# Chunk-selected attention with an ELU MLP on one core: the first block of 384 queries cut into two halves of 192

## The chip, the cores and the metric

The kernel runs on one core of one Trainium2 chip. The metric is the device time of one execution in microseconds (us), as the median over repeated executions. The time before the change is 292.71 us.

## What is computed

The reference is an attention over q, k and v of shape (4, 8, 768, 64) followed by an MLP over 3072 tokens of 512 features, everything given and returned in float32.

```
ub   = sum_d max(q*k_min, q*k_max)        # per query and chunk of 32 keys, 24 chunks
top  = the 6 chunks with the largest ub (chunks after the query's own are excluded)
s    = q @ k.T / 8, kept where the key is not after the query and its chunk is in top
attn = softmax(s) @ v                     # per head
x    = attn, heads side by side           # (3072, 512)
h    = x @ w_in                           # (3072, 2048)
g    = h if h > 0 else exp(h) - 1         # ELU
out  = g @ w_out                          # (3072, 512)
```

A query among the first 192 of its batch (6 chunks of 32) has at most six chunks that are not after it. All of them are in `top`, so for these queries only the causal rule is left.

## The kernel before

**Blocks.** The work is cut into eight blocks (b, h): batch b in 0..3 and half h in 0..1 of its 768 positions, 384 queries each (`HS`). Block i = 2b + h is an attention block and then an MLP block of the same 384 tokens. Heads are taken in four pairs r = 0..3.

**One pair's preparation** (`prep`, with `load`). Six loads of 96 KB bring K, Q and V of the pair's two heads, 384 rows each, into the buffers `kf`, `qf`, `vf`. TensorE transposes K and Q (L468). VectorE takes minimum and maximum of each chunk (L488). `put` (L474 on ScalarE, L476 on VectorE, L478 on GpSimd) makes the bf16 operands `lhs` (keys) and `rhs` (queries) of the scores. A constant pattern of chunks (`econst`, L455/L457) fills the upper half of `lhs` in the first two batches; the selection's mask fills the upper half of `rhs`. One matmul therefore gives the scores with unselected chunks pushed far down. GpSimd casts V into `vext` (L576).

**Selection** (`select`), for two pairs together: the bound as a matmul (L595 in batch 0, L602 later), a transpose (L614), the eight largest per query (L623), a comparison with the sixth (L629), a transpose back (L635), and a copy of the mask into `rhs` (L643, in the operation named `mk`). In blocks with h = 0 it covers only queries 192 to 383.

**Attention** (`attend`) of one pair: scores in segments of key tiles (L673; in the first block a further matmul L678 adds the causal triangle, in later blocks VectorE multiplies by a triangle at L704/L713), exponentials (L689/L695), the product with V (L734), reciprocal and scaling (L745/L748). The result `on` is transposed to `xt`: in the first three blocks by TensorE and a VectorE copy (L769/L772), from the fourth by a DMA transpose on SyncE's queue (L756; the parameter `dx`).

**MLP** (`mlp`): for each of 16 slices of 128 features four matmuls of 384 columns accumulate over the four pairs' `xt` (L784), then exp on ScalarE (L792), min/-1 on GpSimd (L796) and the combination on VectorE (L800) give `gT`. The slices need `xt` of all four pairs. Then for three tiles of 128 tokens sixteen matmuls of 512 columns (L811) give the output, which is copied (L819/L821) and stored. `w_in` and `w_out` are each brought in four DMAs by GpSimd's queue with a cast to bf16 (`load_w_in` L377, `load_w_out` L384). The list `gate` says after how many casts of V each of the eight is issued.

**Order.** A planner (`Graph.run`) lays out all operations at build time with assumed durations, priorities (`att_prio`, `mlp_prio`) and buffer counts (the table `T`), and the program is emitted in the order it found. On the chip each engine runs its list strictly in that order. Where the planner saw TensorE idle it placed an operation `fill` of two matmuls of zeros (L842); a fill is part of TensorE's list and takes its time whether or not it is needed. At most eight loads are under way at once: each load from SyncE's or ScalarE's queue waits for the eighth before it. Eight Q loads, those of the first four pairs, are issued from ScalarE's queue at the start (`nfirst=4`), all other loads from SyncE's.

Of the kernel before, what the change touches and what calls it, by code (L numbers as in the profile page):

```python
# [40 lines left out]
T = dict(kf=6, qf=4, vf=6, pt=10, xt=9, gT=26, xq=2, rhs=7, nfirst=4, vlate=4.68,  # L41
         gate=[2, 3, 5, 5, 6, 6, 8, 10], attw=[7.68, 8.15], mlp=[10.21, 8.14], loada=0.01,
         prepa=4.24, sela=0.01, fill=40, cold=6, evo=0.01, mf=0.3, dx=3,
         slk=[133.66, 359.3, 1054.91, 138.27], sf=0.95, us=1, tp=1, es=0, d1=0)
# [22 lines left out]
class Graph:  # L67
# [41 lines left out]
    def run(self, at=None, dma_lat=(700.0, 900.0)):  # L109
# [8 lines left out]
        flying = [0, 0]  # L118
# [27 lines left out]
        def transfer(t):  # L146
# [3 lines left out]
            while True:  # L150
# [9 lines left out]
                for r, _ in live:  # L160
                    if r[0][1] <= 1e-6:
                        o = r.pop(0)[2]
                        flying[o.engine != POOL] -= 1
                        o.finish = dma_at + dma_lat[1] + o.slack
                        settle(o)
# [9 lines left out]
        while left or any(rings.values()):  # L175
# [13 lines left out]
            while moved:  # L189
                moved = False  # L190
                for e in engines:
# [5 lines left out]
                    while i < len(lst):  # L197
# [4 lines left out]
                        ok = o.xfer is None or e == POOL or flying[1] < 8  # L202
# [32 lines left out]
                    else:  # L235
                        flying[e != POOL] += 1
# [40 lines left out]
def kernel(  # L277
# [45 lines left out]
    slots("gT", T["gT"], [P, HS], BF16)  # L323
# [21 lines left out]
    def consts():  # L345
# [23 lines left out]
        for t in store["selb"]:  # L369
            nc.vector.memset(t, 0.0)  # L370
        for t in store["vext"]:
            nc.gpsimd.memset(t[:, :, :, D:D + 1], 1.0)
# [54 lines left out]

    def load(b, h, r, prio):
# [3 lines left out]
        for buf, src, late in ((kf, k, 0.0), (qf, q, 0.001), (vf, v, T["vlate"])):  # L432
# [9 lines left out]
    def prep(b, h, r, prio):  # L442
# [54 lines left out]
        for hd, rows in enumerate((lo, hi)):  # L497
            put("ka", lambda hd=hd: ap(lb)[lo, hd, ts], lambda rows=rows: ap(kt)[rows],
                c_half(dve=265, pool=560), [(kt, 0)], [(lb, (h, hd))], prio + T["evo"])
# [57 lines left out]
        else:  # L557
# [21 lines left out]
            reads=[(vf, 0), (vf, 1)], writes=[(vx[b, r], h)], prio=prio + T["vlate"]))  # L579

    def select(b, h, gr, prio):
# [56 lines left out]
        for j in range(2):  # L638
            rb = rhs[b, h, prs[j]]

            def mk(e, rb=rb, j=j):
                eng = nc.vector if e == DVE else nc.gpsimd
                eng.tensor_copy(out=ap(rb)[hi, :, q0:HS],  # L643
                                in_=ap(sT)[64 * j:64 * j + 64, 0:nq].rearrange("p (a q) -> p a q", a=1)
                                .to_broadcast([64, 2, nq]))
            g.op("mk" + tag, c_half(dve=2 * nq / 3.84 + 175),
                 mk, reads=[(sT, 0)], writes=[(rb, "mask")], prio=prio, port=True)

    early = [[(0, 0, 128, 0)], [(0, 128, 256, 0), (1, 128, 256, 256)], [(2, 256, 128, 0)]]
# [4 lines left out]
    def attend(b, h, r, prio, w):  # L654
# [4 lines left out]
        todo = early if 2 * b + h < T["es"] and h == 0 else steps[h]  # L659
        nst = len(todo)  # L660
        for si, segs in enumerate(todo):
# [18 lines left out]
            for hd in range(2):  # L680
# [4 lines left out]
                     + ([(ls, ("e", hh)) for hh in range(h + 1)] if b < 2 else []) + [(rs, hd)] + ([(rs, "mask")] if max(c + wd for _k, c, wd, _p in segs) > Q0 else []),  # L685
# [42 lines left out]
        for hd in range(2):  # L728
            def pv(e, hd=hd):
                for qi in range(3):  # L730
# [11 lines left out]
                 writes=[(o3, hd)], prio=pr)  # L742
        rcp, on = g.buf("rcp"), g.buf("on")
        g.op("rcp" + tag, {DVE: (110, 190)},
             lambda e: nc.vector.reciprocal(out=ap(rcp), in_=o3v()[:, :, :, D:D + 1]),  # L745
             reads=[(o3, 0), (o3, 1)], writes=[(rcp, 0)], prio=pr)
        g.op("on" + tag, c_dve(HS),
             lambda e: nc.vector.tensor_tensor(  # L748
                 out=ap(on)[:, :, :, :].rearrange("p q h d -> p h q d"), in0=o3v()[:, :, :, 0:D],
                 in1=ap(rcp)[:, :, :, :].to_broadcast([P, 2, 3, D]), op=AOT.mult),  # L750
             reads=[(o3, 0), (o3, 1), (rcp, 0)], writes=[(on, 0)], prio=pr)
        xt = g.buf("xt")
        xT[b, h, r] = xt
        if 2 * b + h >= T["dx"]:
            def tx(e):
# [3 lines left out]
            g.op("tx" + tag, {SP: (1310, 1310)}, tx, reads=[(on, 0)], writes=[(xt, 0)], prio=pr - 20.0,  # L759
                 xfer=600.0, slack=T["slk"][3])  # L760
            return
        bx = g.buf("bank")

# [3 lines left out]
        def px(e):  # L767
            for qi in range(3):
                nc.tensor.transpose(pxt()[:, P * qi:P * (qi + 1)], ap(on)[:, qi, :, :], ident_b)  # L769
        g.op("px" + tag, c_mm([P] * 3), px, reads=[(on, 0)], writes=[(bx, 0)], prio=pr)  # L770
        g.op("xt" + tag, {DVE: (275, 360)},
             lambda e: nc.vector.tensor_copy(out=ap(xt), in_=pxt()),  # L772
             reads=[(bx, 0)], writes=[(xt, 0)], prio=pr)

    def mlp(i):
        b, h = divmod(i, 2)
        gts = []
        for fc in range(NFC):
            pr = mlp_prio(i, T["mf"] * fc / NFC)
            bank = g.buf("bank")  # L780

            def mm1(e, bank=bank, fc=fc):
                for kk in range(NKK):
                    nc.tensor.matmul(ap(bank)[:, 0:HS], lhsT=w_in_sb[:, kk, P * fc:P * (fc + 1)],  # L784
                                     rhs=ap(xT[b, h, kk]), start=(kk == 0), stop=(kk == NKK - 1))
            g.op(f"h{i}.{fc}", c_mm([HS] * 4), mm1,
                 reads=[(xT[b, h, kk], 0) for kk in range(NKK)] + [(fixed, ("wi", fc // 4))],
                 writes=[(bank, 0)], prio=pr)
            eb, mb, gt = g.buf("e"), g.buf("m"), g.buf("gT")
            gts.append(gt)  # L790
            g.op(f"e{i}.{fc}", c_act(HS),
                 lambda e, eb=eb, bank=bank: nc.scalar.activation(out=ap(eb), in_=ap(bank)[:, 0:HS],  # L792
# [97 lines left out]
```

## Time and profile before

| quantity | value |
|---|---|
| median of 7 runs | 292.71 us (292.4 to 293.96) |
| the profiled execution's own time | 292.6 us |
| its span | 290.9 us |
| TensorE busy | 282.5 us, 97% of the span |
| ScalarE, VectorE, GpSimd busy | 226.9, 216.1, 153.0 us |
| granted TensorE clock over the span | 0.999 |
| HBM read, written | 27.26 MB, 6.29 MB |
| first MLP matmul starts at | 39.0 us |
| last output matmul starts at | 285.8 us |

The 1.7 us between time and span lie outside the profiled instructions. "Busy" of TensorE is the union of records that overlap, and it includes the fills of zeros, so 97% does not say that 97% of the span is useful work. Matmul durations in the profile include the pass through the array; what one costs in a stream is the distance from one start to the next (a row "x4" of 0.65 us has four matmuls 0.162 us apart).

### The profile page before, as it was taken

The numbers are of one execution on the slowest core, as the hardware profiler recorded it, in microseconds if no ns is written. First come the engines' busy times: TensorE is split into PE (matmuls) and PEld (weight loads), VectorE is DVE, ScalarE is ACT, GpSimd is POOL, SyncE is SP. The second block draws the span as 40 slices with busy tenths as digits, with TensorE's granted clock in tenths as the row PEclk, the third lists the DMA queues.
The fourth block names the chain that finished last, engine by engine and source line by source line (L and its number), as shares of the span: only waits on it lengthen the run. The fifth ranks groups of instructions, "written<-read, shape, count | busy, mean of one in ns | idle before, by whom it ended". The sixth has DMA issues, their size and how long they took to land.

```text
span 290.9 us, 7004 instructions
## 1 busy us (share of the span) xinstructions
PE 282.5 (97%) x2288; PEld 170.6 (59%) x2316; DVE 216.1 (74%) x649; ACT 226.9 (78%) x495; POOL 153.0 (53%) x345
## 2 busy tenths in 40 slices
PE   8799999999999999999999999999999999999996
PEld 4467556656565557656565556656665566655542
DVE  8596869897788779777888889778899777623800
ACT  2599799989897699997896799988797978736610
POOL 7585546643489757644485527723385415404700
PEclk9999999999999999999999999999999999999999
DMA  8989998896776785233422523134100210011010
GB/s 169 206 165 220 168 210 156 169 193 133 207 180 147 196 199 123 62 102 99 118 66 68 155 78 71 29 87 108 53 14 18 86 52 14 16 50 75 0 72 37
DMA packets 92836, 31.79 MB, mean 109 GB/s; under 512 B 85632, under 2 KB 89728, under 8 KB 92800
## 3 DMA queue, kind: packets, MB, share of 16 engines
q1 hardware_dynamic: 85376, 26.36, 37.6%
q0 software_dynamic: 4224, 4.19, 9.2%
q10 hardware_dynamic: 3200, 0.79, 1.4%
q8 instruction: 18, 0.29, 0.4%
q14 instruction: 18, 0.15, 0.2%
HBM read 27.26 MB, written 6.29 MB: 115 GB/s over the span
## 4 chain that ended last, share of the span: by engine, by line
PE 87%; DVE 5%; DMA 3%; ACT 2%; issue 1%; ACTq 1%
PE bank L784 28%; PE bank L811 27%; PE bank L673 11%; PE bank L734 7%; PE bank L468 6%; PE bank L842 3%; PE bank L602 2%; DVE kmm L488 2%; DMA qf<-in_q_dram 1%; PE bank L595 1%; DMA vf<-in_v_dram 1%; ACTq L424 1%; ACT pt L689 1%; PE bank L769 1%; DVE thr L623 1%
## 5 line engine op out<-in xcount | busy, mean ns | idle before, releaser
L796 POOL TENSOR_SCALAR m<-e 128x384 f32<-128x384 f32 x128 | 65.3, 522 | 63.9 <-ACT e L792 54.0
L811 PE MATMUL bank<-w_out_sb,gT 128*128 128x512 bf16 x360 | 91.6, 379 | 1.3 <-issue 0.2
L784 PE MATMUL bank<-xt,w_in_sb 128*128 128x384 bf16 x512 | 91.2, 326 | 0.3 <-ACT xq L474 0.2
L800 DVE SCALAR_TENSOR_TENSOR gT<-bank,m 128x384 bf16<-128x384 f32 x128 | 67.3, 554 | 20.7 <-POOL m L796 18.5
L689 ACT ACTIVATE pt<-bank 128x384 bf16<-128x384 f32 (+1 forms) x160 | 75.2, 550 | 7.3 <-PE bank L673 6.4
L784 PEld LDWEIGHTS <-w_in_sb 128*128 128x128 bf16 x512 | 49.2, 98 | 31.9 <-issue 1.9
L792 ACT ACTIVATE e<-bank 128x384 f32<-128x384 f32 x128 | 60.7, 506 | 8.8 <-PE bank L784 6.8
L811 PEld LDWEIGHTS <-gT 128*128 128x128 bf16 x384 | 36.1, 98 | 34.2 <-issue 1.9
L673 PE MATMUL bank<-rhs,lhs 128*128 128x384 bf16 (+2 forms) x288 | 52.9, 290 | 0.1
L478 POOL COPY lhs<-kt 64x384 bf16<-64x384 bf16 x57 | 29.8, 523 | 34.2 <-ACT kt L474 31.9
L488 DVE TENSOR_REDUCE kmm<-bank 128x12 f32<-128x384 f32 x64 | 33.7, 546 | 5.9 <-ACT kt L474 5.2
L673 PEld LDWEIGHTS <-lhs 128*128 128x128 bf16 x288 | 25.5, 98 | 17.5 <-issue 1.8
L819 ACT ACTIVATE o<-bank 128x512 f32<-128x512 f32 x21 | 12.5, 597 | 20.2 <-PE bank L811 18.5
L734 PEld LDWEIGHTS <-pt 128*128 128x128 bf16 x672 | 24.5, 98 | 5.6 <-issue 1.2
L474 ACT ACTIVATE xq<-bank 64x384 f32<-64x384 f32 (+1 forms) x47 | 22.6, 484 | 5.0 <-PE bank L468 3.8
L734 PE MATMUL bank<-vext,pt 128*128 128x65 bf16 x672 | 25.7, 193 | 0.1
L842 PE MATMUL bank<-zeros 128*128 128x512 bf16 x76 | 22.5, 416 | 1.5 <-DVE half L348 1.3
L478 POOL CAST rhs<-xq 64x384 bf16<-64x384 f32 x35 | 18.3, 523 | 8.2 <-ACT xq L474 4.3
L695 ACT ACTIVATE pt<-bank 128x512 bf16<-128x512 f32 x32 | 19.6, 614 | 2.3 <-PE bank L673 2.3
L474 ACT ACTIVATE kt<-bank 128x384 bf16<-128x384 f32 x29 | 14.2, 490 | 6.4 <-PE bank L468 6.4
L576 POOL TENSOR_SCALAR vext<-vf 128x384 bf16<-128x384 f32 x32 | 16.6, 530 | 3.9 <-DMA vf<-in_v_dram 2.4
L748 DVE TENSOR_TENSOR on<-bank,rcp 128x384 bf16<-128x384 f32 x32 | 17.7, 554 | 0.8
(67 smaller groups left out, 271.4 us busy)
## 6 DMA issues: line engine op xcount, KB each, us to landing
kf<-in_k_dram SPq DMA_DIRECT2D x64, 96.0 KB, 2.7
vf<-in_v_dram SPq DMA_DIRECT2D x64, 96.0 KB, 2.6
out_dram<-o SPq DMA_DIRECT2D x24, 256.0 KB, 2.1
qf<-in_q_dram SPq DMA_DIRECT2D x56, 96.0 KB, 2.5
w_in_sb<-in_moe_w_in_dram POOLq DMA_DIRECT2D x4, 512.0 KB, 8.9
w_out_sb<-in_moe_w_out_dram POOLq DMA_DIRECT2D x4, 512.0 KB, 8.6
qf<-in_q_dram ACTq DMA_DIRECT2D x8, 96.0 KB, 3.4
xt<-on SPq DMA_TRANSPOSE x20, 2.3
```

Of the source, the lines that this page charges most:

```text
L474: nc.scalar.activation(out=dst(), in_=src(), func=AF.Copy)
L478: nc.gpsimd.tensor_copy(out=dst(), in_=src())
L488: nc.vector.tensor_reduce(out=ap(kmm)[:, w, :], in_=ap(bank)[:, 0:HS].rearrange("p (c w) -> p c w", w=CHUNK), axis=AX.X, op=op)
L673: nc.tensor.matmul(ap(banks[hd])[:, o + pc:o + pc + wd], lhsT=ap(ls)[:, hd, P * kb:P * (kb + 1)], rhs=ap(rs)[:, hd, c0 - HS * h:c0 - HS * ...
L689: lambda e, hd=hd, pt=pt, banks=banks, wtot=wtot: nc.scalar.activation(out=ap(pt)[:, hd, 0:wtot], in_=ap(banks[hd])[:, 0:wtot], func=AF.Ex ...
L734: nc.tensor.matmul(o3v()[:, hd, qi, :], lhsT=ap(pt)[:, hd, off:off + P], rhs=ap(vx[b, r])[:, kb, hd, :], start=(kb == 0), stop=(kb == qt))
L784: nc.tensor.matmul(ap(bank)[:, 0:HS], lhsT=w_in_sb[:, kk, P * fc:P * (fc + 1)], rhs=ap(xT[b, h, kk]), start=(kk == 0), stop=(kk == NKK - 1))
L792: lambda e, eb=eb, bank=bank: nc.scalar.activation(out=ap(eb), in_=ap(bank)[:, 0:HS], func=AF.Exp),
L796: lambda e, eb=eb, mb=mb: nc.gpsimd.tensor_scalar(out=ap(mb), in0=ap(eb), scalar1=-1.0, scalar2=1.0, op0=AOT.add, op1=AOT.mult),
L800: lambda e, gt=gt, bank=bank, mb=mb: nc.vector.scalar_tensor_tensor(out=ap(gt), in0=ap(bank)[:, 0:HS], scalar=0.0, in1=ap(mb), op0=AOT.max ...
L811: nc.tensor.matmul(ap(bank), lhsT=ap(gts[fc])[:, P * tt:P * (tt + 1)], rhs=w_out_sb[:, fc, :], start=(fc == 0), stop=(fc == NFC - 1))
L842: nc.tensor.matmul(ap(bank), lhsT=zeros[:, 0:P], rhs=zeros, start=True, stop=True)
```

## The change

The first attention block (b = 0, h = 0) is handled by a new function `attend_first`. Each pair is done in two parts: queries 0 to 191, which read no selection mask, and queries 192 to 383, which read it. Each part has its own exponentials, product with V, scaling, TensorE transpose and copy into its half of `xt`. Part 0 has earlier priorities (`a0`, `m0`). The first MLP block is computed in the same halves: one PSUM bank holds two feature slices of 192 tokens each instead of one slice of 384; `gT` becomes a buffer of two slices. The causal triangle is added by matmul in the first two blocks (`tp=2`, before 1), and the DMA transpose starts with the second block (`dx=1`, before 3). Only the first two pairs' Q and K loads are issued first (`nfirst=2`); Q of pairs 2 and 3 moves to SyncE's queue. The table `T` changes throughout: fewer load buffers (K 3 for 6, Q 3 for 4, V 2 for 6), other priorities, and other gates of the weight loads (0, 4, 4, 8, 9, 10, 11, 11 for 2, 3, 5, 5, 6, 6, 8, 10). The planner now models the limit of eight loads by the eighth load before. The mask copy may go to ScalarE in the first block (`fx=2`).

```diff
-T = dict(kf=6, qf=4, vf=6, pt=10, xt=9, gT=26, xq=2, rhs=7, nfirst=4, vlate=4.68,
-         gate=[2, 3, 5, 5, 6, 6, 8, 10], attw=[7.68, 8.15], mlp=[10.21, 8.14], loada=0.01,
-         prepa=4.24, sela=0.01, fill=40, cold=6, evo=0.01, mf=0.3, dx=3,
-         slk=[133.66, 359.3, 1054.91, 138.27], sf=0.95, us=1, tp=1, es=0, d1=0)
+T = dict(kf=3, qf=3, vf=2, pt=8, xt=20, gT=12, xq=6, rhs=5, nfirst=2, vlate=0.74,
+         gate=[0, 4, 4, 8, 9, 10, 11, 11], attw=[8.27, 7.58], mlp=[13.11, 8.2], loada=0.01,
+         prepa=4.3, sela=0.01, fill=45, cold=11, evo=0.01, mf=0.35, dx=1,
+         slk=[129.81, 382.99, 1057.96, 99.72], sf=0.9, us=1, tp=2, d1=2, m0=39.0, a0=34.0, vl0=6.5,
+         fx=2)
...
-                        ok = o.xfer is None or e == POOL or flying[1] < 8
+                        ok = (o.xfer is None or e == POOL or len(issued) < 8
+                              or (issued[-8].finish or 1e12) - issued[-8].slack <= t)
...
+    def attend_first(r, prio, w):
+        tag = f"00{r}"
+        ls, rs = lhs[0, r], rhs[0, 0, r]
+        parts = (([(0, 0, Q0, 0), (1, P, 64, Q0)], [(0, P, 0), (Q0, 64, 0)],
+                  [[(0, 0)], [(0, P), (1, Q0)]]),
+                 ([(0, Q0, Q0, 0), (1, Q0, Q0, Q0), (2, 2 * P, P, 2 * Q0)], [(Q0, 64, 64), (2 * Q0, P, 0)],
+                  [[(0, 0), (1, Q0)], [(0, 64), (1, Q0 + 64), (2, 2 * Q0)]]))
+        for part, (segs, diag, tiles) in enumerate(parts):
+            pr = prio + w * 0.5 if part else prio - T["a0"]
+            pt = g.buf("pt" if part else "pa")
...
+                     reads=[(ls, (0, hd)), (ls, ("e", 0)), (rs, hd)] + ([(rs, "mask")] if part else []),
...
+            turn(0, 0, r, o3, 2, part + 1, pr)
...
+        for f2 in range(NFC // 2):
+            if i:
...
+                continue
+            for part in range(2):
+                pr = mlp_prio(0, T["mf"] * f2 / (NFC / 2)) - (0 if part else T["m0"])
+                bank = g.buf("bank")
+                for x in range(2):
+                    mm1(bank, 2 * f2 + x, Q0 * x, Q0 * part, Q0, x, pr)
...
-            for _ in range(2):
+            for _ in range(1 if cold else 2):
                 nc.tensor.matmul(ap(bank), lhsT=zeros[:, 0:P], rhs=zeros, start=True, stop=True)
-        cost = 860 if i < T["cold"] else 432
+        cost = 430 if cold else 432
```

## The prediction

> **What bounds the kernel now.** I read the page's busy shares and slices first, then busy time by stage, then who waits for whom in the first 40 us, then the DMAs in two stretches, then the timeline. From the page (engine, busy us, share; then 40 slices of 7.3 us in tenths):
>
> ```profile
> span 290.9 us, 7004 instructions
> PE 282.5 (97%) x2288; PEld 170.6 (59%) x2316; DVE 216.1 (74%) x649; ACT 226.9 (78%) x495; POOL 153.0 (53%) x345
> ...
> ACT  2599799989897699997896799988797978736610
> ...
> DMA  8989998896776785233422523134100210011010
> ```
>
> TensorE is the bound after the start. ScalarE is nearly full from slice 3 to slice 8, and the DMA engines are full to about 60 us. By stage (busy us of PE, PEld, DVE, ACT, POOL; clock; DMA share; GB/s):
>
> ```profile
> 0.00:14.50 14.50, 11.62 (x50) 6.29 (x50) 9.71 (x31) 5.62 (x12) 8.88 (x35) 1.00 0.96 187
> 14.50:39.00 24.50, 23.91 (x212) 15.43 (x215) 19.50 (x76) 22.27 (x47) 17.21 (x36) 1.00 1.01 186
> 39.00:56.00 17.00, 16.89 (x157) 10.58 (x157) 15.14 (x45) 16.57 (x38) 8.60 (x18) 1.00 0.95 179
> 56.00:76.00 20.00, 19.01 (x186) 11.69 (x189) 15.95 (x48) 17.45 (x38) 9.83 (x22) 1.00 0.85 160
> 76.00:286.00 210.00, 208.76 (x1680) 125.77 (x1698) 155.75 (x452) 164.41 (x363) 108.46 (x236) 1.00 0.33 86
> ```
>
> After 76 us TensorE is idle 1.2 us in 210, so only the first 76 us have time to give. Their busy share hides zeros. The groups of the first 60 us show it (loads of weights are counted in full; four matmul records are missing):
>
> ```profile
> L842 PEld LDWEIGHTS <-zeros 128*128 128x128 bf16 x64 | 6.3, 106 | 6.3 <-issue 2.5 <-DVE half L348 1.3
> ```
>
> 64 matmuls of zeros at 0.216 us (start to start) are 13.8 us, all ahead of the first MLP matmul at 39.0 us. The waits from 5 to 40 us (waiter <- releaser: us, times, longest):
>
> ```profile
> POOL lhs L478 <- ACT kt L474: 4.0, 2, 2.6
> DVE kmm L488 <- ACT kt L474: 3.5, 2, 2.8
> ACT xq L564 <- DMA vf<-in_v_dram: 3.2, 1, 3.2
> ```
>
> ScalarE stands 3.2 us before the relu at 10.77 because its queue holds the eighth Q load until a V load (the eighth before it) has landed. GpSimd and VectorE wait behind it, and TensorE stands 0.86 and 0.76 us. Last, the DMA issues between 8 and 18 us and between 19 and 29 us (KB, median us to landing):
>
> ```profile
> vf<-in_v_dram SPq DMA_DIRECT2D x7, 96.0 KB, 2.7
> kf<-in_k_dram SPq DMA_DIRECT2D x6, 96.0 KB, 2.7
> ...
> w_in_sb<-in_moe_w_in_dram POOLq DMA_DIRECT2D x2, 512.0 KB, 7.9
> kf<-in_k_dram SPq DMA_DIRECT2D x4, 96.0 KB, 6.3
> qf<-in_q_dram SPq DMA_DIRECT2D x4, 96.0 KB, 6.6
> ```
>
> Loads issued beside two weight DMAs land 4 us later than the others.
>
> **The change part by part.** Durations are of the profiled execution (292.6 us, span 290.9; the median is 0.1 above). Counts are from the two programs' instruction lists.
>
> *TensorE's content ahead of the last output product.* Fills: 70 before, 65 after (14 stand behind it, 10 before): -5 x 0.216 = -1.08. Products with V: 16 more of 65 columns at 0.030 = +0.48. Triangles: from 24 of 128 columns to 40 of 128 and 16 of 64: +16 x 0.056 + 16 x 0.031 = +1.39. Transposes of `on`: from 36 to 16: -1.12. Scores recut in the first block: +0.05. First MLP block: 64 matmuls of 384 columns (0.162) become 128 of 192; 192 columns are not in the trace and lie midway between 128 (0.056) and 256 (0.109), 0.0825: 10.56 for 10.37, +0.19. Sum -0.1. The list is no shorter; any gain must come from waits.
>
> Here a rule speaks against the change. Matmuls of 65 columns, each with its own weight load, are 0.030 us apart (rows "x30" of 0.91 us), those of 512 columns 0.216. The Trainium skill, "TensorE: Matmul & The Clock Gate", section "Back-to-back issue gap", says that in a stream of weight loads and matmuls both set the spacing, about 81 ns at 128 columns and 131 at 512. An estimate from it, on the line between, is 89 ns at 192 and 114 at 384: 11.4 for 7.3, +4.1 us, and the forecast would be 294.8. I take +0.19, since the trace has the weight load hidden even at 65 columns; bounds 0 and +4.1.
>
> *Waits up to the first MLP matmul.* Before: content 17.0 + 13.8 of fills = 30.8, start at 39.0, so 8.2 us are lost: 1.26 before the first matmul, 2.7 at the cold start (ten fills at 0.43 for 0.216, two transpose groups at 0.85 instead of 0.49), 4.2 in waits. After: content 15.4 + 11.0 (51 fills) = 26.4. The start costs 1.26 + 2.5 again (nine fills). Two waits change:
> - ScalarE issues four Q loads instead of eight, none held: its 3.2 us stand goes. The Q loads of pairs 2 and 3 go to SyncE's queue behind K loads, at 0.53 us each; they cost nothing while the transposes that read them come later in TensorE's list (content 7.8 and 10.6, estimated landing 8.5 and 10.3 us).
> - The first weight DMA has no gate and is GpSimd's first work after the constants. It occupies GpSimd for about 0.9 us (row L377: 0.75 to 0.98), from 7.8 to 8.7. Queued behind it are the two casts of K (L478, 0.5 each) that the first scores read, ready at 9.2 and 9.7. TensorE reaches these scores at content 3.8 + 1.26 + 2.5 = 7.5: it waits about 2.2. ScalarE's next copies wait for the Q transpose behind these scores.
>
> I put the later waits of the start at 0.5 (bounds 0 and 2.0, what is now lost beyond those named). Lost: 1.26 + 2.5 + 2.7 = 6.5 for 8.2: -1.7; the first MLP matmul starts at about 32.9.
>
> *ScalarE as a check.* Its list up to the last exp of the first MLP block has 44.5 us of work before and ends at 56.1; after it is 47.3 (more scores of the second block come ahead). Before it started at 5.4 (table loaded) and lost 6.2, 3.2 of them at that load. After it can start at 4.3 and loses 3.0: 54.6, where TensorE's content is 60.6, as before at 56.1 (60.7). That is -1.5. Both say the same; I take -1.7.
>
> *Edits with no price of their own.* VectorE gains four more reciprocals, scalings and copies (4 x about 0.6) and loses the eight `xt` copies of blocks 1 and 2 (0.36 each) and the four triangles of the second block (0.72): about -3.3 of 216, at 75 to 90% busy. Split outputs of `gT` and the wider `pa` cost as the present rearranged ones (L748, 554 ns, as L800); bound 0 to +0.3. Eight more DMA transposes take SyncE's queue 1.2 us each and land in 2.3 (row of `xt`), 10 us before the MLP that reads them by TensorE's list; beside weight DMAs they may take 7, still covered. If SyncE holds there, loads queue behind it, and with three K buffers the cover is two pairs. The mask copy on ScalarE is one operation of 0.45. The fills behind the last product end near 289.0, when the last store lands: 0 to +0.2.
>
> Sum: -0.1 - 1.7 = -1.8: 290.8 of 292.6, as a median 290.9.
>
> **The rivals.**
>
> *The gain is given back between 33 and 76 us* (chance 0.18). ScalarE is 97% busy from 39 to 56 us and has more in its list there; with K, Q, V buffers halved, less is loaded ahead. If about 1.5 of the 1.8 comes back as waits, the time is 292.4. For it: 1.0 us of idle TensorE now between 56 and 76. Against: ScalarE's list ends earlier by my sum.
>
> *The weights' stretch catches the ninth pair's K* (slower, 0.26). The second and third quarter of `w_in` are issued together, after the cast of the fourth pair's V: I estimate 26.0 us. (That V is the 39th and 40th load. Loads issued after 8 us land behind the first quarter of `w_in`, near 7.8 + 6.7 = 14.5, 6.7 being the fastest landing of such a DMA here; from there SyncE issues one per 0.53 us and each lands 2.5 us later: near 24.9, then the cast and one more copy.) Before, the pair issued at 18.96 ended at 29.04, 10.1 later; loads issued after it landed between or behind. The ninth pair's K is estimated to be issued at 25.0 to 26.1, so the margin is under 1 us. It stands in TensorE's list just ahead of the first MLP matmul. Caught behind both weights it lands near 36.4, where TensorE wants it at 32.6: +3.8, so 292.6 - 1.8 + 3.8 = 294.6, as a median 294.7; caught between them, +1 and within the first rival. It decides if the issue comes later than GpSimd's second quarter. For it: the 4 us in the two DMA rows above. The skill's "DMA: Bandwidth & Descriptors", section "Queues, rings and completion order", says each DMA engine goes round between queues packet by packet; by that the load would lose well under 1 us in its own turn, and the time would be 290.9 in this case too. The rows decide: it stays, at 294.7.
>
> *The waits nearly all go* (0.10). With 0.5 instead of 2.7 us lost in waits: 288.7.
>
> *The change doesn't do what it says:* the lists do hold the halves and the early scores without a mask; but part 1 follows so closely (scores of both parts of pair 0 are 8 us apart) that part 0 may bring no MLP forward. That is the first rival's number.
>
> **How the numbers follow.** The likeliest case, 0.46, gives 290.9 (own range 289.6 to 291.8). With the others: 288.7 (0.10), 292.4 (0.18), 294.7 (0.26, up to 297). 0.3%, about 0.9 us, is what a measurement of this kernel can tell from no change; faster means under 291.8: 0.46 + 0.10 = 0.56; within: 0.18; slower: 0.26. The range for 8 in 10 is 288.5 to 295.0: it leaves out the upper part of the slower case and the lowest edge.
>
> **What would show it.** Right: the first MLP matmul near 33; no wait of ScalarE for a load near 10 us; a wait of TensorE of about 2 us near 8 us with the K cast on GpSimd as releaser; the ninth pair's K landing by 29 us; the same idle after 76 us. Wrong: TensorE standing before 192-column matmuls with nothing waited for (the spacing rule), a first MLP matmul after 35 with a K load as releaser, or new idle TensorE after 76 us through K, V or DMA transposes that come late.

## The result, and the profile after

The changed kernel takes 290.68 us (median of 23 runs, 289.18 to 292.94); the kernel before, run beside it, 292.43 us (median of 60, 291.2 to 293.96). The ratio is 0.9932, 95% interval 0.9917 to 0.9947. It is faster by 1.75 us, where the forecast said 1.8. The profiled execution took 289.84 us. In what follows a stand is time in which an engine does nothing but wait for what its next operation needs.

From its page (engine, busy us, share; then slices of 7.2 us in tenths):

```profile
span 288.1 us, 7248 instructions
PE 281.3 (98%) x2398; PEld 175.5 (61%) x2423; DVE 210.8 (73%) x652; ACT 221.3 (77%) x486; POOL 154.4 (54%) x348
...
ACT  4778989997587989986598889995798879814610
...
DMA  8977999999485746447742433315400111002001
```

ScalarE starts earlier (first two slices 4 and 7 for 2 and 5); the DMA engines stay nearly full to 72 us. The busy times by stage:

```profile
0.00:14.50 14.50, 11.64 (x68) 6.58 (x70) 10.56 (x42) 9.04 (x16) 10.44 (x39) 1.00 0.95 178
14.50:39.00 24.50, 23.89 (x265) 17.73 (x266) 20.86 (x84) 21.26 (x46) 15.31 (x33) 1.00 0.87 172
39.00:56.00 17.00, 17.00 (x240) 14.71 (x238) 14.00 (x42) 16.00 (x39) 11.18 (x24) 1.00 1.05 178
56.00:76.00 20.00, 18.67 (x170) 10.88 (x170) 14.23 (x51) 15.30 (x33) 9.85 (x23) 1.00 0.98 163
76.00:286.00 210.00, 208.87 (x1663) 125.17 (x1680) 151.11 (x438) 159.68 (x355) 107.60 (x232) 1.00 0.36 92
```

ScalarE does 9.04 us of work in the first 14.5 us where it did 5.62. The last row is as before (208.87 of 210 for 208.76): the gain lies in the first 76 us. TensorE's busy share hides it again, since fills of zeros count as work. I therefore take, at a landmark, the time minus the list's content up to there (each matmul at its start-to-start distance, fills included), and call the rest lost. Before and after, in us:

| landmark | time | content | lost |
|---|---|---|---|
| ninth group of K/Q transposes | 16.51, 19.02 | 9.46, 13.79 | 7.05, 5.24 |
| first MLP matmul | 39.00, 32.14 | 30.73, 26.28 | 8.27, 5.86 |
| last matmul of the first block's first MLP layer | 55.23, 55.01 | 46.45, 48.22 | 8.78, 6.79 |
| first MLP matmul of the second block | 76.32, 76.19 | 66.06, 67.61 | 10.26, 8.58 |
| last first-layer matmul of all | 274.19, 272.23 | 261.33, 261.14 | 12.86, 11.09 |

The lists hold the same (-0.19 at the end); 1.8 us fewer are lost. (The two profiled executions differ by 2.8 us, 0.8 of it after the last product, which the medians do not show.) Of the 1.8, nearly all is there at the ninth group of transposes, before any half of the MLP has begun. The waits from 5 to 40 us (waiter <- releaser: us, times, longest):

```profile
POOL lhs L486 <- ACT kt L482: 2.3, 2, 1.7
...
DVE kmm L496 <- ACT kt L482: 1.7, 1, 1.7
PE bank L821 <- POOL lhs L486: 1.5, 1, 1.5
```

ScalarE's first relu, at 10.77 us before, now runs at 6.61:

```profile
6.61 0.36 ACT L572 ACTIVATE xq<-xq 128x192 f32<-128x192 f32 x1 [0.43 <-DVE xq L484]
```

ScalarE's wait of 3.2 us for a V load is gone, and what stood behind it on GpSimd and VectorE is half as long. In its place TensorE waits for the K casts that are queued behind the first weight DMA on GpSimd. Four rows of TensorE's timeline (start, us, ..., [idle before <- releaser]):

```profile
8.71 0.26 PE L821 MATMUL bank<-rhs,lhs 128*128 128x192 bf16 x1 [1.54 <-POOL lhs L486]
...
32.14 1.07 PE L883 MATMUL bank<-xt,w_in_sb 128*128 128x192 bf16 x11
...
36.03 0.67 PE L883 MATMUL bank<-xt,w_in_sb 128*128 128x192 bf16 x6 [0.51 <-DMA w_in_sb<-in_moe_w_in_dram]
...
68.59 0.52 PE L476 MATMUL bank<-ident_f,kf 128*128 128x128 f32 x3 [1.18 <-DMA kf<-in_k_dram]
```

Eleven matmuls of 192 columns take 1.07 us, the last 0.246 of it its own pass: 0.082 us from start to start. The last two rows are new stands on loads. The DMA issues from 27 to 38 us (KB, median us to landing):

```profile
w_in_sb<-in_moe_w_in_dram POOLq DMA_DIRECT2D x2, 512.0 KB, 8.5
qf<-in_q_dram SPq DMA_DIRECT2D x4, 96.0 KB, 7.1
kf<-in_k_dram SPq DMA_DIRECT2D x4, 96.0 KB, 4.8
vf<-in_v_dram SPq DMA_DIRECT2D x4, 96.0 KB, 7.2
```

The pair of weights was issued at 28.72 and 29.55 us, the ninth pair's K at 27.95 and 28.43: K landed at 30.56 and 30.96, just ahead of the weights, and what was issued after it (Q, V) waited 7 us.

### The profile page after: what moved, and what is told of

Same layout as the page of the kernel before. It is cut to its first block, busy times and chain, and to the rows that moved or that the text cites. A ratio compares the mean times of both kernels' runs of the same rounds, so it can differ in the third digit from the quotient of the medians.

```text
span 288.1 us, 7248 instructions
## 1 busy us (share of the span) xinstructions
PE 281.3 (98%) x2398; PEld 175.5 (61%) x2423; DVE 210.8 (73%) x652; ACT 221.3 (77%) x486; POOL 154.4 (54%) x348
## 4 chain that ended last, share of the span: by engine, by line
PE 89%; DMA 5%; POOL 2%; DVE 2%; issue 1%; SPq 0%; POOLq 0%
PE bank L883 29%; PE bank L915 27%; PE bank L683 11%; PE bank L744 6%; PE bank L476 6%; PE bank L952 4%; PE bank L610 3%; DMA w_in_sb<-in_moe_w_in_dram 3%; DMA kf<-in_k_dram 2%; PE bank L603 1%; PE bank L821 1%; POOL econst L359 1%; PE bank L825 0%; POOL kst L370 0%; PE bank L849 0%
## 5 line engine op out<-in xcount | busy, mean ns | idle before, releaser
L883 PE MATMUL bank<-xt,w_in_sb 128*128 128x384 bf16 (+1 forms) x576 | 93.8, 308 | 0.5 <-DMA w_in_sb<-in_moe_w_in_dram 0.5
L699 ACT ACTIVATE pt<-bank 128x384 bf16<-128x384 f32 (+1 forms) x152 | 71.1, 546 | 5.2 <-PE bank L683 4.8
L883 PEld LDWEIGHTS <-w_in_sb 128*128 128x128 bf16 x576 | 53.5, 98 | 28.8 <-issue 1.2
L864 ACT ACTIVATE e<-bank 128x384 f32<-128x384 f32 x128 | 60.7, 510 | 10.2 <-PE bank L883 8.1
L683 PE MATMUL bank<-rhs,lhs 128*128 128x384 bf16 (+2 forms) x264 | 49.6, 292 | 0.0
L683 PEld LDWEIGHTS <-lhs 128*128 128x128 bf16 x264 | 23.8, 98 | 16.4 <-issue 1.8
L924 ACT ACTIVATE o<-bank 128x512 f32<-128x512 f32 x18 | 10.7, 596 | 27.9 <-PE bank L915 27.9
L744 PEld LDWEIGHTS <-pt 128*128 128x128 bf16 x624 | 22.5, 97 | 5.3 <-issue 1.6
L744 PE MATMUL bank<-vext,pt 128*128 128x65 bf16 x624 | 23.6, 193 | 0.0
L767 DVE TENSOR_TENSOR on<-bank,rcp 128x384 bf16<-128x384 f32 (+1 forms) x36 | 18.6, 520 | 0.6
L705 ACT ACTIVATE pt<-bank 128x512 bf16<-128x512 f32 x28 | 17.7, 631 | 1.6 <-PE bank L683 1.3
```

The lines of the kernel that those rows point to most:

```text
L683: nc.tensor.matmul(ap(banks[hd])[:, o + pc:o + pc + wd], lhsT=ap(ls)[:, hd, P * kb:P * (kb + 1)], rhs=ap(rs)[:, hd, c0 - HS * h:c0 - HS * ...
L699: lambda e, hd=hd, pt=pt, banks=banks, wtot=wtot: nc.scalar.activation(out=ap(pt)[:, hd, 0:wtot], in_=ap(banks[hd])[:, 0:wtot], func=AF.Ex ...
L744: nc.tensor.matmul(o3v()[:, hd, qi, :], lhsT=ap(pt)[:, hd, off:off + P], rhs=ap(vx[b, r])[:, kb, hd, :], start=(kb == 0), stop=(kb == qt))
L864: lambda e: nc.scalar.activation(out=ap(eb), in_=ap(bank)[:, 0:HS], func=AF.Exp),
L883: nc.tensor.matmul(ap(bank)[:, o:o + wd], lhsT=w_in_sb[:, kk, P * fc:P * (fc + 1)], rhs=ap(xT[b, h, kk])[:, c0:c0 + wd], start=(kk == 0), ...
```

## The experiments

Each kernel ran beside the kernel before on the same chip, whose median there was 292.66 to 293.49; times are medians, ratios against those runs with 95% intervals (a ratio is not exactly the quotient of the two medians).

**The changed kernel again.** Unchanged.

> The changed kernel once more, as the base of the other runs and for a second profile. My theory (gain from the waits ahead of the first MLP matmul): the first MLP matmul starts near 32.1 us again and the time is 1.5 to 2.0 us under the kernel before. The rival (the weights' stretch catches the ninth pair's K in some executions): the issue of that K is so near to that of the second weight DMA that in another execution it may land after 33 us, and the first MLP matmul then starts at 33 to 37.

290.23, ratio 0.9903 (0.9869 to 0.9937). Its profiled execution took 291.45, 1.6 more than the first one. To the first MLP matmul both are alike (32.16 us, lost 5.88); then TensorE stood twice:

```profile
36.51 1.49 PE L883 MATMUL bank<-xt,w_in_sb 128*128 128x192 bf16 x16 [0.97 <-DMA w_in_sb<-in_moe_w_in_dram]
...
40.93 0.32 PE L683 MATMUL bank<-rhs,lhs 128*128 128x384 bf16 x1 [1.09 <-DVE gT L876]
```

The first stand is for the weights themselves (the second quarter of `w_in`). The second comes from V: the seventh pair's V, issued 29.25 and 29.73 beside the weights, landed at 35.96 and 38.46 (in the other execution 32.9 and 36.52). Its cast heads GpSimd's queue; the `m` behind it is late, then `gT`, then the bank. So the weights' race with the loads costs about 0.5 us in one execution and 2 in another. That is the difference between these two; for the kernel's other executions, 289.18 to 292.94, it is not shown.

**The Q loads alone, in the kernel before.** Its order is kept; only the queue changes:

```diff
         for o in order:
-            o.emit(o.engine)
+            late_q = o.xfer is not None and o.engine == ACT and o.name in ("ld002", "ld003")
+            o.emit(SP if late_q else o.engine)
```

> The kernel before, its planned order untouched, but the Q loads of pairs 2 and 3 are issued from SyncE's queue at the same place in the overall order. One part of the change alone. My prediction's theory (ScalarE's stand of 3.2 us is what costs TensorE its waits): ScalarE's wait at 10.8 us is gone, TensorE's two waits of 0.9 and 0.8 us near 11 to 13 us go, and the time falls by 1.0 to 1.7 us. Rival (the stand is cover: TensorE's list has fixed fills and the DMA's supply of K and Q sets the pace): ScalarE's wait goes, the first MLP matmul moves by less than 0.4 us, and the time stays within 0.4 us of the kernel before.

296.57, ratio 1.0114 (1.0072 to 1.0156): slower. ScalarE's stand is gone and the ninth group of transposes starts 2.9 us earlier (13.61, lost 4.16), but all of it and more is lost afterwards. TensorE's timeline:

```profile
26.35 0.87 PE L468 MATMUL bank<-ident_f,kf 128*128 128x128 f32 x3 [6.23 <-DMA kf<-in_k_dram]
```

The V casts that gate the first pair of weights also come earlier, so the pair goes out at 15.78 us instead of 18.96. The sixth pair's K, issued 16.56 and 17.09, is caught behind it and lands at 23.57 and 26.21. What each theory expected was missed. That the weights are the cause is argued here from the trace; the two edits together, below, show it.

**The first weight DMA later.** In the changed kernel, on GpSimd's queue:

```diff
+    move(named("w_in0")[0], named("ka000")[1])    # behind the first two K casts
```

> The changed kernel, but GpSimd issues the first quarter of w_in behind its two first casts of K instead of ahead of them; nothing else in any list moves. My theory: TensorE's wait of 1.5 us at 8.7 us (on the cast on GpSimd) shrinks to under 0.7, and since TensorE's list is fixed everything behind it moves up by about 1 us; the first MLP matmul near 31.1 and the time 0.7 to 1.2 us under the changed kernel. Rival (the wait is repaid by the next one, because loads and ScalarE set the pace to 30 us): the first MLP matmul stays at 31.8 to 32.2 and the time within 0.3 us of the changed kernel.

290.13, ratio 0.9899 (0.9872 to 0.9926), as the unchanged kernel in the same comparison. The wait near 8 us shrinks and the first MLP matmul comes 0.85 us earlier (31.30), as the theory said, but the time does not follow. The stand behind `gT` is there again, since a half of the seventh pair's V landed only at 36.84; it was in one of the two profiles of the unchanged kernel too, so that V gives the whole gain back is not shown:

```profile
7.72 0.26 PE L821 MATMUL bank<-rhs,lhs 128*128 128x192 bf16 x1 [0.62 <-POOL lhs L486]
...
39.31 0.32 PE L683 MATMUL bank<-rhs,lhs 128*128 128x384 bf16 x1 [1.09 <-DVE gT L876]
```

**No fills after the cold start.** 34 fill operations of the changed kernel are left out; they compute nothing that is used.

```diff
-            o.emit(o.engine)
+            if o.name != "fill" or o in fills[:T["cold"]]:
+                o.emit(o.engine)
```

> The changed kernel with the 34 later fills (68 matmuls of zeros, 14.7 us of TensorE's list) not emitted; the eleven at the start stay. It leaves out only work that the output does not need. My theory (fills mostly lie in waits that would be there anyway, but a part of them delays what comes next): the granted clock stays 1.0 after the start, idle TensorE replaces the zeros, and the time falls by 0.3 to 1.0 us. Rival A (fills are wholly cover): within 0.3 us. Rival B (without them the clock is taken back in the gaps of the first 30 us): more matmuls at the doubled spacing and 1 to 4 us more.

290.55, ratio 0.9898 (0.9866 to 0.9931): the same time. The first MLP matmul comes at 31.52, 0.6 earlier, although its list there is 8.6 us shorter. So nearly all of the removed fills had filled waits. By stage:

```profile
0.00:14.50 14.50, 9.76 (x60) 6.05 (x61) 10.94 (x43) 9.02 (x16) 10.67 (x39) 1.00 0.95 176
14.50:29.10 14.60, 11.94 (x171) 9.30 (x169) 13.20 (x51) 12.50 (x27) 8.50 (x18) 1.00 0.76 171
29.10:43.70 14.60, 10.32 (x82) 7.37 (x83) 10.06 (x36) 11.65 (x26) 7.80 (x18) 0.88 0.91 167
```

TensorE is idle 4.3 us of 14.6 in the third row (a stand of 2.93 us among them), and the granted clock there is 0.88; with the fills it is 1.00.

**Weights earlier.** The price of the second rival: in the changed kernel the second and third quarter of `w_in` ahead of the cast of the fourth pair's V.

```diff
+    v3 = named("v003")[0]
+    move(named("w_in1")[0], v3, False)
+    move(named("w_in2")[0], v3, False)
```

> The changed kernel with the weight quarters two and three of w_in issued on GpSimd's queue ahead of the cast of the fourth pair's V, which is near 25.2 us instead of 28.72 and 29.55 us; everything else keeps its order. The weights' rival says that the ninth pair's K (issued 27.95 to 28.91, landed 30.56 and 30.96 in the changed kernel) and the eighth pair's loads are then caught between the two weight transfers, land 4 to 5 us later, and TensorE stands 2 to 5 us on K near 33 us: 292.5 to 295. The theory that the head is bound by TensorE's list alone says 290.7 within 0.5, since the weights only come sooner.

296.69, ratio 1.016 (1.0117 to 1.0203): 6.0 us above the changed kernel's 290.68, and above both theories' ranges. The pair went out at 25.36 and 26.19; the ninth pair's K, issued 28.55 and 29.19, landed at 36.12 and 36.57, the eighth Q just before:

```profile
35.84 0.52 PE L476 MATMUL bank<-ident_f,qf 128*128 128x128 f32 x3 [4.64 <-DMA qf<-in_q_dram]
```

```profile
PE   8899399999999999999999999999999999999998
...
PEclk9999979999999999999999999999999999999999
```

In the slice after the stand (the 3 of the first row) the clock is 0.7 to 0.8.

**A K half ahead of the DMA transpose.** In the changed kernel, on SyncE's queue near 59 us:

```diff
+    tx = named("tx012")[0]
+    k_half = next(o for o in order[order.index(tx):] if o.engine == SP and o is not tx)
+    move(tx, k_half)
```

> The changed kernel with one step of SyncE moved: the K half that is issued at 61.54 us behind the DMA transpose (59.29 to 61.49 on SyncE) is issued ahead of it, so that it is on its way before the w_out pair (issued 58.27 and 59.10). Theory: the stand of 1.18 us at 68.59 goes and nothing takes its place, since 76 us onward is full: 289.5 (1.2 less). Rival: the transpose comes 1 us later and its reader or the next K stands instead: 290.7 within 0.3.

289.98, ratio 0.991 (0.9878 to 0.9943). The stand at 68.59 is gone from the trace (the second profile of the unchanged kernel has one of 1.04 us there), and no stand over 0.2 us is named between 42 and 78 us. The median is 0.7 under one of the unchanged kernel's two medians and 0.25 under the other (290.68, 290.23): the trace shows the wait removed, the times do not prove its worth. The edit brings the K half ahead of the transpose and of the `w_out` pair at once, so which of the two had delayed it is not separated.

**The V cast later as well.** The same, and the seventh pair's V cast moved behind the next two `m` on GpSimd:

```diff
+    v7 = named("v012")[0]
+    ms = [o for o in order[order.index(v7):] if o.name.startswith("m0.")][:2]
+    move(v7, ms[1])
```

> The changed kernel with the K half issued ahead of the DMA transpose near 59 us, as in the experiment that did this alone (289.98), and the seventh pair's V cast on GpSimd moved behind the next two of the ELU's m, so that a V load that lands at 38 us holds up only its own product. Theory: the stand of 1.25 us at 39.7 us (TensorE for a bank held by gT, which waits for m behind the V cast) goes: 288.7 to 289.5. Rival: the V cast is now late for its own PV product or frees its load buffer later, and the stand moves there: 290 within 0.4.

290.01, ratio 0.9906 (0.988 to 0.9931). The stand behind `gT` is gone, the one for the weights' own quarter is not (0.92 at 36.47 us, with `w_in` as releaser), and the time is that of the kernel with the K half alone. The rival's number holds, but not its reason: the profiled execution (289.28) has no other stand over 0.2 us between 37 and 78 us. Why the medians do not show the removed stand stays open.

**The new numbers without the halves.** The changed code and table, but the first block attended and multiplied whole, planned anew:

```diff
-            if i:
-                attend(b, h, r, att_prio(i, 0.25 * r), 0.25 * w)
-            else:
-                attend_first(r, att_prio(i, 0.25 * r), 0.25 * w)
+            attend(b, h, r, att_prio(i, 0.25 * r), 0.25 * w)
...
         for f2 in range(NFC // 2):
-            if i:
+            if True:
```

> The changed kernel's code and planner numbers without the halves: the first block is attended and fed to the MLP whole, as before the change (its selection rows are waited for), planned anew. TensorE's content ahead of the first MLP matmul is 34.5 us here against 26.3 with the halves. Theory that the halves carry the gain: the first MLP matmul near 42 us, the cover for the waits between 26 and 42 us is missing, 293 to 296. Rival, that the new numbers of the table (load buffers, first pairs, order of V) carry it: 290 to 291.5.

290.78, ratio 0.993 (0.9899 to 0.9961): all of the gain, without the halves. My theory in this expectation is wrong. The first MLP matmul comes at 39.89 us, as late as before:

```profile
L883 PE MATMUL bank<-xt,w_in_sb x22: 323/326/326, 39.9 to 45.9; 128*128 128x384 bf16 x22
```

Up to there 34.48 us of content (14.88 of it fills) and 5.42 lost, where the halves have 26.28 and 5.86. The early MLP halves take the place of fills, and the two times differ by less than the runs can tell. At the ninth group of transposes 4.62 us are lost, before the change 7.05: the gain sits at the same place as in the changed kernel.

**The halves with the old numbers.** The changed code with the kernel before's buffers, gates and `nfirst=4`, planned anew (the halves' own `m0`, `a0` kept, `vl0=4.68`, `fx=0`, `gT=13`):

```diff
-T = dict(kf=3, qf=3, vf=2, pt=8, xt=20, gT=12, xq=6, rhs=5, nfirst=2, vlate=0.74,
-         gate=[0, 4, 4, 8, 9, 10, 11, 11], attw=[8.27, 7.58], mlp=[13.11, 8.2], loada=0.01,
+T = dict(kf=6, qf=4, vf=6, pt=10, xt=9, gT=13, xq=2, rhs=7, nfirst=4, vlate=4.68,
+         gate=[2, 3, 5, 5, 6, 6, 8, 10], attw=[7.68, 8.15], mlp=[10.21, 8.14], loada=0.01,
...
```

> The halves with the planner numbers of the kernel before (more buffers for loads, four first pairs, V 4.68 us later than K, first weight transfers sooner), planned anew. Content ahead of the first MLP matmul 25.2 us. Theory that the halves carry the gain: the first MLP matmul at 31 to 34 us and 290 to 291.5. Rival, that the halves need the new table: the weight quarters are issued while K and V of pairs five to nine are still to come, stands of 3 us and more between 25 and 45 us, and 293 to 296.

294.76, ratio 1.0065 (1.0041 to 1.0089): slower. The first MLP matmul comes at 33.49, as the theory said, with 8.41 us lost before it. ScalarE's stand is back, and here the early scores pay for it; ScalarE's rows and TensorE's:

```profile
10.26 0.37 ACTq L429 DMA_DIRECT2D qf<-in_q_dram  x1
10.68 0.36 ACT L572 ACTIVATE xq<-xq 128x192 f32<-128x192 f32 x1 [3.30 <-DMA vf<-in_v_dram]
11.05 0.52 ACT L482 ACTIVATE rhs<-xq 64x384 bf16<-64x384 f32 x1
...
11.62 0.32 PE L821 MATMUL bank<-rhs,lhs 128*128 128x192 bf16 x1 [2.45 <-ACT rhs L482]
```

An early first MLP matmul is thus neither needed for the gain nor enough for it. The loss goes on growing after 90 us in this kernel; the cause of that is open.

**Q loads and weights, each alone and both, in the kernel before.** Its order is kept but for these edits: the Q loads of pairs 2 and 3 issued from SyncE (as above), and the first pair of `w_in` moved:

```diff
+    ka = named("ka011")[1]           # K copies of the sixth pair
+    move(named("w_in1")[0], ka)
+    move(named("w_in0")[0], ka)
```

Both edits:

> The kernel before in its own order with two edits: the Q loads of the third and fourth pair are issued from SyncE at the places where ScalarE issued them, and the first pair of w_in transfers is moved on GpSimd's queue behind the K copies of the sixth pair. With the first edit alone the 24th transpose came 2.9 us sooner, but the weights were issued at 15.78 us, caught the K loads issued 16.56 and 17.09 and cost 6.2 us. Theory, from the whole first block with the new planner numbers giving 290.8: the gain is ScalarE's stand taken away with the weights kept behind the loads, and the halves are not needed for it: 289.8 to 291.2. Rival, that the new table's order of V and its buffers are needed too: the 2.9 us are given back before 45 us at V or at the second weight quarters, 292 to 293.5.

The second alone:

> The kernel before with the second of the last experiment's two edits alone: the first pair of w_in transfers moved on GpSimd's queue behind the K copies of the sixth pair (here about 23.7 us instead of 18.96), the Q loads of the third and fourth pair still issued from ScalarE. Together the two edits gave 289.55, the Q loads alone 296.57. Theory, that ScalarE's stand carries the gain and the place of the weights only keeps it: the 24th transpose stays near 16.5 us and the time at 292 to 293.5, no gain. Rival, that the place of the weights carries it: 290 to 291.

| Q loads of pairs 2 and 3 | weights in their place | weights later |
|---|---|---|
| from ScalarE | 1 (292.4 to 293.5) | 292.66, ratio 0.9997 (0.9973 to 1.0021) |
| from SyncE | 296.57, ratio 1.0114 (1.0072 to 1.0156) | 289.55, ratio 0.9887 (0.986 to 0.9915) |

Both together give 3.1 us; the weights' place alone gives nothing, and the Q loads alone lose. ScalarE with both edits and with the weights alone:

```profile
6.92 0.49 ACT L474 ACTIVATE xq<-bank 128x384 f32<-128x384 f32 x1 [2.43 <-PE bank L468]
7.44 0.36 ACT L564 ACTIVATE xq<-xq 128x192 f32<-128x192 f32 x1
```

```profile
10.30 0.46 ACTq L424 DMA_DIRECT2D qf<-in_q_dram  x1
10.81 0.36 ACT L564 ACTIVATE xq<-xq 128x192 f32<-128x192 f32 x1 [3.26 <-DMA vf<-in_v_dram]
```

The relu that stood behind the held Q load comes at 7.44 instead of 10.81. The weights' place is in the next rows, one kernel each: Q loads alone, both, weights alone (ns to issue; first and last start of the four `w_in` DMAs):

```profile
L377 POOL DMA_DIRECT2D w_in_sb<-in_moe_w_in_dram x4: 750/788/986, 15.8 to 37.7; - x4
```

```profile
L377 POOL DMA_DIRECT2D w_in_sb<-in_moe_w_in_dram x4: 750/788/986, 21.2 to 31.1; - x4
```

```profile
L377 POOL DMA_DIRECT2D w_in_sb<-in_moe_w_in_dram x4: 750/788/986, 24.9 to 33.8; - x4
```

With both edits one stand of 1.40 us on K remains (21.94 us). 4.58 us are lost at the ninth group of transposes, 7.20 at the first MLP matmul, 10.72 at the last (before 7.05, 8.27, 12.86). With the weights alone the time is as expected, but that group came at 17.80, not at 16.5. TensorE stood for the held Q load, and what came next ran at about half its pace:

```profile
13.69 0.90 PE L468 MATMUL bank<-ident_f,qf 128*128 128x128 f32 x3 [1.15 <-DMA qf<-in_q_dram]
```

The same group of three takes 0.55 us in the kernel before's profile, after a stand of 0.76; from 14 to 18 us the granted clock is 0.62 here and 1.00 there. Up to 18 us the two kernels have the same order. Of the 66 executions of the kernel before that ran beside these experiments, 24 have a mean granted clock of 0.994, as this one has, and took 293.37 to 294.13 us; the median of the other 42 is 292.42. In the changed kernel it is one of 24, with both edits none of 6. So the stands seem to have a second price, about 1.3 us in a third of the executions; only this one trace shows where the clock falls. The 1.75 us of the medians are without it (292.42 to 290.68).

**The Q loads back on ScalarE, in the changed kernel.**

```diff
+        late_q = [o for n in ("ld002", "ld003")
+                  for o in sorted((x for x in g.ops if x.name == n), key=lambda x: x.seq)[2:4]]
         for o in order:
-            o.emit(o.engine)
+            o.emit(ACT if o in late_q else o.engine)
```

> The changed kernel in its own order with the Q loads of the third and fourth pair issued from ScalarE again, at the places where SyncE issued them. Theory of ScalarE's stand: the issues wait for earlier landings (6.5 to 8 us), the rhs copies behind them (6.88 us here) come 1 to 1.5 us later, TensorE's first half scores of 8.7 us with them, and 291.2 to 292.5 result. Rival, that the halves' early work hides the stand: 290.7 within 0.4.

292.59, ratio 0.9995 (0.9975 to 1.0016): the whole gain is gone. The profiled execution was the longest of twelve (296.43; it stood twice on K, 4.4 us in all), so only its start is read, which comes before those stands: ScalarE's queue, then TensorE's.

```profile
9.57 0.37 ACTq L429 DMA_DIRECT2D qf<-in_q_dram  x1
9.99 0.52 ACT L482 ACTIVATE rhs<-xq 64x384 bf16<-64x384 f32 x1 [1.81 <-PE bank L476]
...
10.56 0.24 PE L821 MATMUL bank<-rhs,lhs 128*128 128x192 bf16 x1 [1.10 <-ACT rhs L482]
```

The second `rhs` copy of the first pair, done by 7.9 us in the changed kernel, waits behind a Q load that ScalarE can issue only at 9.57. That load was held by two things that ended together: an older K load, landed at 9.47, and the Q transposes on TensorE, ended at 9.46, which the row names and which free its buffer (the new table has three for Q). TensorE stands 1.10 us for it, and 6.66 us are lost at the ninth group for 5.24. The stand is what the change removes, with halves or without.

## Why the prediction was right, and where it was not

**TensorE's list, -0.1: right.** The content at the end is 0.19 us shorter. 192 columns cost 0.082 to 0.083 us, as interpolated (0.0825). The rule on the spacing of matmuls, weighed and set aside in the prediction, (the Trainium skill, "TensorE: Matmul & The Clock Gate", section "Back-to-back issue gap"), would have shown as wider spacing: at 192 columns its estimate was 0.089 us, and the median start-to-start distance in the trace is 0.083; at 384 it was 0.114, and the trace has 0.162.

**Waits up to the first MLP matmul, 6.5 instead of 8.2: right in kind, 0.6 too high.** 5.86 and 5.88 us are lost in two executions, and the matmul starts at 32.14 instead of the forecast 32.9. ScalarE's stand went, as said. Up to the first scores at 8.71 us the forecast's terms are 1.26, 2.5 for the cold start and 2.2 for GpSimd's K casts; they measured 1.26, 1.96 and 1.70 from start to start (1.54 of it idle). The "later waits of the start", put at 0.5, measured 0.9. So the waits gave 2.4 us up to there and not 1.7, and 0.7 was lost again after it (below): that the total comes within 0.1 us of the forecast is luck.

**What carries the gain: the sum was right, and the experiments narrow it.** The prediction gave the halves themselves next to nothing (-0.1) and everything to ScalarE's stand. The runs agree: without the halves the gain stays (290.78), with the Q loads back on ScalarE it goes (292.59), and in the kernel before the stand's removal with the weights held back brings at least as much as the whole change (289.55). What it did not say is the condition. Taking the stand away moves the gates of the weights forward too, and alone that made the kernel slower (296.57). In the changed kernel the new gates keep the pair of weights back to 28.72 us.

**ScalarE as a check, 54.6 us for the last exp of the first MLP block: wrong.** It ended at 57.17, 1.0 us later than before (56.15), while TensorE had lost 2 us less. The list of ScalarE does not bound this stretch; that the two sums agreed was chance. The step that failed is "loses 3.0": started at 4.29 with the 47.3 us of work counted in the prediction, it lost 5.6. What it lost more is mostly waits for TensorE: up to that exp they come to 5.3 us where before they were 3.2 (3.2 and 2.9 of them for banks of K and Q transposes). Waits for VectorE, 0.8, are new. The TensorE contents set beside this check, 60.7 and 60.6 us, cannot be right, since they exceed the time that had passed; the table above has 46.45 of 55.23 us and 48.22 of 55.01.

**The rival of the weights' stretch: right mechanism, wrong time and price.** The pair was estimated at 26.0 us and came at 28.72. The V cast that gates it began at 26.70 (V had landed late), and the "one more copy" behind it waited another 1.07 us for VectorE:

```profile
26.70 0.51 POOL L584 TENSOR_SCALAR vext<-vf 128x384 bf16<-128x384 f32 x1 [1.55 <-DMA vf<-in_v_dram]
28.28 0.50 POOL L486 COPY lhs<-kt 64x384 bf16<-64x384 bf16 x1 [1.07 <-DVE kt L484]
28.72 1.58 POOL L382 DMA_DIRECT2D w_in_sb<-in_moe_w_in_dram  x2
```

The ninth pair's K was late by as much (27.95 for 25.0), so the margin was as thin as foreseen and K passed. What was caught instead was V, which cost nothing in one execution and 1.09 us in the other; the weights' own quarter came 0.5 and 1.0 us late for TensorE. Moved 3.4 us forward, the pair did catch K: it landed at 36.12 and 36.57, the forecast said 36.4. But the price was 6.0, not 3.8. Two things had been left out: the eighth Q was caught too and held TensorE first (4.64 us), and the clock fell after the stand (mean 0.95 from 14.5 to 39 us). The choice of the DMA rows over the rule of turns holds, as far as the prediction's reading of that rule goes ("well under 1 us", for which it gave no working): K, Q and V loads beside a pair of weights took 4.8 to 9.3 us to land (medians by tensor in the changed kernel, with the weights earlier, and with the Q loads alone).

**Given back between 33 and 76 us: in part.** From the first MLP matmul to that of the second block the profiled execution lost 2.7 us, 0.7 more than before (2.0); the second one lost 4.3. One of the steps said where it might be: loads queued behind a DMA transpose on SyncE. The K half issued at 61.54, behind a transpose from 59.29 to 61.49, cost 1.18 us in the trace. It was also beside the `w_out` pair (issued at 58.27 and 59.10) and took 6.9 us to land.

**Idle after 76 us: the same**, 1.13 us for 1.24.

## What to carry to other kernels

A load that is issued from a compute engine's queue and must wait for an older transfer (here the eighth before it) holds that engine's next operation until that one has landed; look for a compute operation whose releaser is a load that it does not read, and move the issue to a queue that computes nothing. When a stand near the start goes, ask which gates move forward with it: bulk weights that go out earlier can land ahead of the loads that the bound engine wants next, and the two edits must be made together (-3.1 us), since the first alone cost 3 us. A restructuring that starts the main work 7 us sooner gained nothing that could be told here (290.68 with it, 290.78 without), since it only took the place of filler.

## What the runs showed of the hardware that was not expected

At the start of a pair of 512 KB weight DMAs (issued at 28.72 us in the changed kernel) one microsecond decides a load's fate: the K half issued at 28.43 landed after 2.5 us, the V halves issued at 29.01 and 29.49 after 3.9 and 7.0. In the second execution (weights at 28.75) a K half issued at 28.66 landed after 2.4, the V half at 29.25 after 6.7.

Stands of TensorE of 4.6 and 6.2 us were followed by a lower granted clock (0.7 to 0.8 in the following slice after 4.64 us, 0.6 to 0.7 in the slice at the 6.23 us stand); so was a stretch without fills that holds a stand of 2.93 us (0.88 over 14.6 us). So were, in the kernel before with the weights later, two stands of 1.00 and 1.15 us within 2.7 us (0.62 from 14 to 18 us). A stand can then cost more than its own length: with the Q loads alone, the time between the ninth group of transposes and the first MLP matmul (at 44.49 us) grew by 8.4 us, with a stand of 6.23 in it. At which length the clock falls is not shown: other stands of 1.0 to 1.6 us left it at 1.00.
